# Batch 0's transforms in fp32, a first chunk fed with uncentred tokens, and staged weight sums in three buffers

## The chip, the cores and the metric

The kernel runs on one core of a Trainium2 chip. The metric is the device time of one execution in microseconds, lower is better. Three runs of the kernel before took 1044.42, 1047.3 and 1050.25 us, so its median is 1047.3 us.

## The reference, cut to what matters

Eight batches of 576 tokens with 512 channels. Pooled attention gives x; two Fourier transforms are added to it; an MLP on the normalised sum follows.

```python
k_p, v_p = means of k and v over 8 neighbouring tokens
x  = softmax(q @ k_p.T / sqrt(64)) @ v_p
u  = x + real(fft(fft(x, axis=tokens), axis=channels))
un = (u - mean(u)) / sqrt(var(u) + 1e-6)
out = u + relu(un @ w_ch1) @ w_ch2          # 512 -> 2048 -> 512
```

## The kernel before, in words

**MLP in blocks.** The 4608 tokens are cut into nine blocks of 512. The hidden layer has 16 chunks f of 128. Every operand is split into a high part of type fp32r and a low part, so a product is three fp32r matmuls (high by high, high by low, low by high). Blocks 0 and 1 are computed by `plain` (L889): per chunk twelve fp32r matmuls into `g` (L897), then a ReLU on ScalarE (L902), the low part `hl` on VectorE (L903) and twelve matmuls into `acc` (L861). Blocks 2 to 8 use a Strassen-like scheme with seven products per pair of chunks (L965).

**Front end.** `fe(b)` (L334) computes batch b up to the operands of its block: scores (`psS`, L440), softmax, transposes (`psT`, `psV`, `psR`), values (`psX`), then the two transforms by matmuls with cosine and sine tables. Sums `tmpE` (L618) and differences `tmpO` (L631) of mirrored tokens are split (`split`, L606 to L611), multiplied by `ca` (`psA` L652, `psB` L669), the results are split again (`parts`, `parts_last`, L635 to L642, and L658), and multiplied by `cb` (`psQ`, `psP`, L686). VectorE adds the results to x (L694, L695, L703, L704), forms the sum `s` (L715), the sums and differences U (L722, L723), and, with the mean from a matmul (`psM`, L763), the centred X (L770). `centre` (L727) makes the parts `un0h` on ScalarE (L732) and `un0l` on VectorE or POOL (L733). The lists UE and UL say how many of the four U operations and of the four low parts are on VectorE for batch 0, batch 1 and the others; the rest are on POOL.

**Weights.** The weights come as 64-bit numbers. `prep_w(n)` (L192) turns a piece into fp32 by two ScalarE operations (L203, L205) and one of VectorE (L208), then into its two parts (L215, L218); pieces are taken alternately from the two matrices. `HOLD` names for some pieces the instruction behind which ScalarE's part is queued. The weights of the first matrix are also written to the buffer `w1d` in device memory.

**Staged sums.** Blocks 2 to 8 need sums of neighbouring weight chunks. `load_pair(j)` (L231) brings chunks 2j and 2j+1 from `w1d` into one half of the buffer `sx`, `combine(j)` (L234) forms the sums by four VectorE operations (L238 to L241), splits them on ScalarE and POOL (L244, L245; the high parts go into the other half of `sx`), and writes them to `w1s`. Its last statement is `load_pair(j + 1)`, so a pair is loaded when the one before it has been written out:

```python
        if j + 1 < NFC // 2:
            load_pair(j + 1)
```

**Order.** A planner orders each engine's instructions by its own times; from position 86 of the main loop on, TensorE's order is the order of the program. Positions count the steps of `fast()`. The lists AT1 to AT7 say at which position each step of the front ends of batches 1 to 7 is issued, PAIRS at which a `combine` is. The two loads of `ca` and `cb` are issued on POOL's queue early in batch 0. `keep_busy` puts matmuls on TensorE whose result is not used (L325): 4 after batch 0's values and 5 after its mean.

Of the kernel before, what the change touches and what calls it, by code (L numbers as in the profile page):

```python
# [41 lines left out]

HZ = {0, 1}

DG = {0, 1}


UE = [4, 4, 2]
UL = [3, 3, 2]

AHEAD, WBUFS, LOOK = 10, 12, 9
HOLD = {0: ("B", 0), 1: ("S", 1, 0, 0), 2: ("S", 1, 0, 1), 4: ("T", 1, 0), 6: ("R", 1, 0), 8: ("S", 1, 1, 0), 10: ("S", 1, 1, 1)}
# [3 lines left out]
UNITS0, UNITS, TAIL = 90, 104, (2, 8, 14, 20, 26)  # L56
MANUAL = 86
PAIRS = [95, 110, 119, 136, 136, 145, 158, 174]
# [34 lines left out]
def tile_kernel(ctx: ExitStack, tc: tile.TileContext, qt, kt, vm, vr, w1, w2, cad, cbd, mkd, out):  # L93
# [20 lines left out]
    ss = cb[:, 1450:2890].rearrange("p (a n) -> p a n", a=5)  # L114
    mk = cp.tile([P, 5], F32, name="mk")
# [34 lines left out]
    for t in kpb:  # L150
        nc.gpsimd.memset(t, 0.0)
    for t in rw:
        nc.scalar.copy(out=t, in_=zz[:96, :P])
    nc.scalar.copy(out=xe, in_=zz[:, :290])

    for _ in range(4):
        nc.tensor.matmul(warm, lhsT=zz[:, 0:P], rhs=zz[:, 0:512], start=True, stop=True)

# [13 lines left out]
    highs = {}  # L172
# [19 lines left out]
    def prep_w(n):  # L192
# [3 lines left out]
        if wide:  # L196
            st = staged.pop(n)
            hi = st[:, :, :, 1]
            d0 = wd[3 * i + f % 3]
            di = d0.bitcast(I32).rearrange("p (r x) -> p r x", r=2)  # L200

            with tc.issue_after(behind[HOLD[n]].ins) if n in HOLD else ExitStack():
# [4 lines left out]
            with tc.issue_after(behind["Bv" if n < 3 else "C", 0].ins) if n < 6 else ExitStack():  # L207
                nc.vector.scalar_tensor_tensor(out=di, in0=hi, scalar=3, in1=di, op0=ALU.logical_shift_left, op1=ALU.bitwise_or)  # L208
        else:
            d0 = staged.pop(n)  # L210
        if i == 0:
# [5 lines left out]
        with queued(("C", 0) if n < 6 else None):  # L217
            nc.vector.tensor_tensor(out=lw, in0=d0, in1=raw(wh), op=ALU.subtract)  # L218
# [11 lines left out]

    def load_pair(j):  # L231
        nc.sync.dma_start(sx[:, 0:2 * DM].rearrange("p (f n) -> p f n", f=2), w1d[:, 2 * j:2 * j + 2])

    def combine(j):  # L234

        x, y = sx[:, 0:DM], sx[:, DM:2 * DM]
# [5 lines left out]
        for n, t in enumerate((x, y)):  # L242
            h = sx[:, (2 + n) * DM:(3 + n) * DM]
# [4 lines left out]
        if j + 1 < NFC // 2:  # L248
            load_pair(j + 1)
# [70 lines left out]
    def keep_busy(ins, n):  # L320

        with tc.issue_after(ins.ins):
            ps = bank(0, "idle")
            for _ in range(n):
                nc.tensor.matmul(ps, lhsT=ident, rhs=raw(ca)[:, 0:512], start=True, stop=True)  # L325
# [8 lines left out]
    def fe(b):  # L334
# [35 lines left out]
        def prep_k(g):  # L370
            ks = wk.tile([P, J], F32, tag="ks", name="ks")
            kb = kpb[g % 2]
            with queued({(1, 0): ("f", 0), (1, 1): ("f", 0)}.get((b, g))):
                total(ks, st["k", g], PK)
            with tc.issue_after(behind["R", 0, 0].ins) if b == 1 and g == 3 else ExitStack():
# [3 lines left out]
        def prep_rem(gi):  # L379
            vt = wk.tile([32, D], F32, tag="vt", name="vt")  # L380
# [3 lines left out]
        def prep_v(gi, i):  # L384
# [771 lines left out]
```

## Time and profile before

| | |
|---|---|
| median of three runs | 1047.3 us |
| the profiled execution | 1051.85 us |
| its span, first to last instruction | 1050.1 us, 1.75 us less |
| mean granted TensorE clock | 0.981 of 2.4 GHz |
| TensorE busy | 1003.6 us |
| VectorE, ScalarE, POOL busy | 692.2, 566.7 and 440.7 us |

Engine names in the rows: PE is TensorE's matmul, PEld its weight load, DVE is VectorE, ACT is ScalarE, POOL is GpSimd, SP the queue that issues most transfers. A stretch of the table of windows is given from the span's start in us. A busy PE is a modelled figure. The granted clock is 1.00 at 2.4 GHz and 0.50 at 1.2 GHz. A matmul on fp32 operands has two records, one on fp32r has one.

### The profile page before, as it was taken

The numbers are of one execution on the slowest core, as the hardware profiler recorded it, in microseconds if no ns is written. First come the engines' busy times: TensorE is split into PE (matmuls) and PEld (weight loads), VectorE is DVE, ScalarE is ACT, GpSimd is POOL, SyncE is SP. The second block draws the span as 40 slices with busy tenths as digits, with TensorE's granted clock in tenths as the row PEclk, the third lists the DMA queues.
The fourth block names the chain that finished last, engine by engine and source line by source line (L and its number), as shares of the span: only waits on it lengthen the run. The fifth ranks groups of instructions, "written<-read, shape, count | busy, mean of one in ns | idle before, by whom it ended". The sixth has DMA issues, their size and how long they took to land.

```text
span 1050.1 us, 18757 instructions
## 1 busy us (share of the span) xinstructions
PE 1003.6 (96%) x5982; PEld 866.0 (82%) x5982; DVE 692.2 (66%) x1387; ACT 566.7 (54%) x1687; POOL 440.7 (42%) x461
## 2 busy tenths in 40 slices
PE   7869999899889999999999999999999999999998
PEld 4547778677768799897899889998989988999897
DVE  6798686676579657965787668756875686223222
ACT  5769673556455756665567556755664344222222
POOL 5623333246533563556435743554351234222221
PEclk8989999899899999999999999999999999999999
DMA  7579997678856777878678757876787578888884
GB/s 272 183 227 390 374 320 257 197 256 254 258 153 188 232 256 207 259 234 279 189 235 275 256 186 231 284 230 213 219 258 215 174 237 286 274 256 263 288 257 135
DMA packets 161458, 256.11 MB, mean 244 GB/s; under 512 B 15952, under 2 KB 73296, under 8 KB 161104
## 3 DMA queue, kind: packets, MB, share of 16 engines
q1 hardware_dynamic: 161072, 252.24, 75.0%
q0 software_dynamic: 288, 2.66, 0.7%
q8 instruction: 49, 0.80, 0.3%
q14 instruction: 49, 0.40, 0.1%
HBM read 217.63 MB, written 37.22 MB: 243 GB/s over the span
## 4 chain that ended last, share of the span: by engine, by line
PE 76%; DVE 9%; DMA 7%; ACT 3%; POOL 2%; issue 2%; SPq 1%; DVEq 0%; POOLq 0%; ACTq 0%
PE acc L861 33%; PE x L965 23%; PE g L897 6%; PE psX L524 3%; PE psS L440 3%; DMA sx<-w1d 2%; PE psP L686 2%; DMA w1s<-sx 2%; PE psA L652 1%; ACT t L447 1%; PE psT L476 1%; PE psB L669 1%; PE psQ L686 1%; DMA v<-in_vm 1%; DMA k<-in_kt 1%
## 5 line engine op out<-in xcount | busy, mean ns | idle before, releaser
L926 DVE TENSOR_TENSOR sx<-x,sx 128x256 f32<-128x256 f32 x336 | 154.7, 464 | 163.3 <-PE x L965 153.1
L936 POOL TENSOR_TENSOR hl<-sx,hh 128x512 fp32r<-128x512 f32 x112 | 150.8, 1347 | 225.7 <-ACT hh L935 184.0
L965 PE MATMUL x<-un0h,w1op 128*128 128x256 f32 x896 | 173.6, 282 | 2.1 <-ACT U L527 1.6
L861 PE MATMUL acc<-hh,w2low 128*128 128x512 f32 x576 | 165.2, 400 | 0.0
L934 ACT ACTIVATE sx<-sx 128x512 f32<-128x512 f32 x112 | 71.0, 634 | 165.7 <-DVE sx L926 163.3
L965 PEld LDWEIGHTS x<-un0h,w1op 128*128 128x128 f32 x896 | 143.0, 189 | 14.9 <-ACT U L527 2.3
L965 PE MATMUL x<-un1h,w1op 128*128 128x256 f32 x672 | 135.0, 283 | 1.2 <-DVE sx L926 1.1
L965 PEld LDWEIGHTS x<-un1h,w1op 128*128 128x128 f32 x672 | 111.2, 189 | 13.6 <-DVE sx L926 2.0
L861 PEld LDWEIGHTS acc<-hh,w2low 128*128 128x128 f32 x576 | 101.6, 190 | 16.1 <-issue 0.4
L861 PE MATMUL acc<-hh,w2high 128*128 128x512 f32 x360 | 104.7, 398 | 1.1 <-ACT hh L935 1.1
L861 PE MATMUL acc<-hl,w2high 128*128 128x512 f32 x360 | 103.0, 395 | 0.0
L965 PE MATMUL x<-un0l,w1op 128*128 128x256 f32 x448 | 88.4, 279 | 0.0
L447 ACT ACTIVATE t<-psS,mx 128x72 f32<-128x72 f32 x240 | 74.3, 337 | 12.7 <-DVE mx L442 12.2
L861 PEld LDWEIGHTS acc<-hh,w2high 128*128 128x128 f32 x360 | 63.1, 189 | 11.1 <-ACT hh L935 1.8
L861 PEld LDWEIGHTS acc<-hl,w2high 128*128 128x128 f32 x360 | 63.2, 189 | 10.2 <-DVE w2low L218 0.4
L935 ACT CAST hh<-sx 128x512 fp32r<-128x512 f32 x112 | 69.7, 623 | 2.8
L965 PEld LDWEIGHTS x<-un0l,w1op 128*128 128x128 f32 x448 | 68.1, 188 | 0.0
L965 PE MATMUL x<-un1l,w1op 128*128 128x256 f32 x336 | 66.5, 279 | 0.0
L368 POOL TENSOR_TENSOR v<-v 128x256 f32<-128x256 f32 (+1 forms) x56 | 52.9, 945 | 30.6 <-DMA v<-in_vm 29.6
L456 POOL TENSOR_TENSOR t<-t,sm 128x720 f32<-128x720 f32 x30 | 44.9, 1499 | 43.3 <-DVE sm L455 11.7
L861 PE MATMUL acc<-hl,w2h 128*128 128x512 f32 x216 | 61.0, 402 | 0.0
L861 PE MATMUL acc<-hh,w2h 128*128 128x512 f32 x216 | 59.3, 395 | 0.0
(267 smaller groups left out, 2085.1 us busy)
## 6 DMA issues: line engine op xcount, KB each, us to landing
w1op<-w1s SPq DMA_DIRECT2D x224, 256.0 KB, 3.4
w1op<-w1p SPq DMA_DIRECT2D x200, 256.0 KB, 3.6
w2low<-w2l SPq DMA_DIRECT2D x128, 256.0 KB, 3.5
w2high<-w2d SPq DMA_DIRECT2D x80, 256.0 KB, 3.6
U<-in_w SPq DMA_DIRECT2D x16, 512.0 KB, 6.1
sx<-in_w SPq DMA_DIRECT2D x16, 512.0 KB, 6.0
w1s<-sx SPq DMA_DIRECT2D x32, 256.0 KB, 3.6
k<-in_kt SPq DMA_DIRECT2D x28, 288.0 KB, 3.7
```

The source lines that it names most:

```text
L368: nc.gpsimd.tensor_tensor(out=out if n == 1 else src[:, :, 0:n], in0=src[:, :, 0] if n == 1 else src[:, :, 0:n], in1=src[:, :, 1] if n == ...
L440: nc.tensor.matmul(ps[:, c * W2J:(c + 1) * W2J], lhsT=q[:, r0:r0 + P], rhs=kpb[g % 2], start=True, stop=True)
L447: behind["S", b, gi, i] = nc.scalar.activation(t[:, c0 + c, h], pv[:, c, h], AF.Exp, bias=mx[x], accum_out=sm[x])
L456: ins = nc.gpsimd.tensor_tensor(out=t, in0=t, in1=sm.unsqueeze(3).broadcast_to([P, 5, 2, J]), op=ALU.mult)
L686: nc.tensor.matmul(ps, lhsT=w, rhs=a, start=(i == 0), stop=(i == 6))
L861: nc.tensor.matmul(acc[e], lhsT=a[:, e], rhs=h, start=(f == 0 and x == 0), stop=(f == NFC - 1 and x == 2))
L897: nc.tensor.matmul(ps, lhsT=w[:, c], rhs=x[:, ti], start=(n == 0), stop=(n == 11))
L926: nc.vector.tensor_tensor(out=o, in0=x, in1=y, op=ALU.add)
L934: nc.scalar.activation(c, c, AF.Relu)
L935: nc.scalar.copy(out=h, in_=c)
L936: nc.gpsimd.tensor_tensor(out=l, in0=c, in1=raw(h), op=ALU.subtract)
L965: nc.tensor.matmul(ps, lhsT=w[:, q, i], rhs=y[:, c + i], start=(n == 0), stop=(n == 5))
```

## The change

- Batch 0's transforms (`NF`): the sums and differences of tokens go into the matmuls as fp32, with fp32 tables `cf` and `sf` that are loaded in the place of `ca` and `cb`. Both splits are gone; 30 fp32 matmuls in tiles of 96 tokens take the place of 74 fp32r ones: nine for `psA` (three of them with 128 columns), six for `psB`, six for `psQ`, nine for `psP`. Six ScalarE copies bring the results of the first transform to SBUF. The loads of `ca` and `cb` are issued at position 7 of the main loop instead.
- The first chunk of block 0 (`WHOLE = 1`): its weights stay whole in fp32 and are multiplied by U, the tokens with their mean on, by four fp32 matmuls; a fifth one takes the mean off: the sums of the weights over channels (`ws`, one VectorE reduction, and `psW`, one small matmul) times the token sums `s`.
- `KB = [4, 0]`: the five idle matmuls after batch 0's mean are gone.
- `UE` from [4, 4, 2] to [2, 3, 2] and `UL` from [3, 3, 2] to [0, 3, 2]; of the two L618 additions of batch 0 one goes to POOL (`FP`).
- Staged sums: pairs are loaded into six 512-column tiles, which give three places; three pairs are loaded ahead; the high parts have two places in `sx`.
- One of batch 1's four softmaxes (`SMX`) takes its exponentials straight from PSUM with ScalarE's own sums: VectorE's two subtractions (L449) and one reduction (L453) become ScalarE operations.
- Conditions of the order: L208 of the first three pieces waits for batch 0's last L631 instead of L637; eight `PINS`; five entries of AT3 four positions earlier, five of AT2 one earlier, five of PAIRS one later.

Renamed tiles and parts that are only moved are left out of this cut:

```diff
+SMX = {(1, 1, 0)}
+FP = {(0, 1)}
+PINS = [
+    ('Activation', 'un0h3', 0, 't3_1', 6),
+    ('DVE', 'hl', 12, 'AB2_1', 1),
+    ('DVE', 'nt2', 1, 'al3_2', 0),
+    ('DVE', 'xe', 2, 'rw1', 6),
+    ('DVE', 'sm1_1', 0, 'w2low', 3),
+    ('Activation', 'wdh', 0, 'wh1_3', 2),
+    ('Pool', 'wlo3_0', 0, 't3_0', 0),
+    ('Activation', 'wf3_3', 0, 'rw1', 7),
+]
+LEAD = 3
+KB = [4, 0]
-UE = [4, 4, 2]
-UL = [3, 3, 2]
+NF = {0}
+WHOLE = 1
+STEP = 96
+CONSTS = 7
+UE = [2, 3, 2]
+UL = [0, 3, 2]
-PAIRS = [95, 110, 119, 136, 136, 145, 158, 174]
+PAIRS = [95, 110, 119, 137, 137, 146, 159, 175]
-AT3 = [-46, -40, -37, -33, -33, -20, -18, -15, -15, -7, -7, -7, -7, 13, 13, 13, 13, 15, 15, 17, 18, 21, 21, 21, 21,
+AT3 = [-46, -40, -37, -33, -33, -24, -22, -19, -19, -11, -7, -7, -7, 13, 13, 13, 13, 15, 15, 17, 18, 21, 21, 21, 21,
...
-AT2 = [-6, 6, 8, 8, 8, 17, 18, 21, 22, 23, 24, 26, 27, 27, 29, 31, 32, 34, 35, 38, 39, 42, 43, 43, 44, 44, 52, 52,
-       52, 57, 59, 60, 61, 61, 61, 63, 65, 66, 70, 70, 70, 78, 78, 78, 78, 78, 80, 99]
+AT2 = [-6, 6, 8, 8, 8, 17, 18, 21, 22, 23, 24, 26, 27, 27, 29, 31, 32, 34, 35, 38, 38, 41, 42, 43, 44, 44, 52, 52,
+       52, 57, 59, 60, 61, 61, 61, 63, 64, 65, 70, 70, 70, 78, 78, 78, 78, 78, 80, 99]
...
     def prep_w(n):
...
+        if i == 0 and f < WHOLE:
+            ws = wk.tile([P, P], F32, tag="wf", bufs=2, name=f"ws{f}")
+            with queued(ORB.get(n)):
+                nc.vector.tensor_reduce(out=ws, in_=d0.rearrange("p (c m) -> p m c", m=P), op=ALU.add, axis=AX.X)
+            ps = bank(0, f"psW{f}")[:, 0:P]
+            nc.tensor.matmul(ps, lhsT=raw(avg), rhs=ws, start=True, stop=True)
+            nc.scalar.mul(wm[:, f], ps, -1.0)
...
+    halves = [(wd[0], wd[1]), (wd[3], wd[4]), (wd[2], wd[5])]
     def load_pair(j):
-        nc.sync.dma_start(sx[:, 0:2 * DM].rearrange("p (f n) -> p f n", f=2), w1d[:, 2 * j:2 * j + 2])
+        for n, t in enumerate(halves[j % 3]):
+            nc.sync.dma_start(t, w1d[:, 2 * j + n])
     def combine(j):
-        x, y = sx[:, 0:DM], sx[:, DM:2 * DM]
+        x, y = halves[j % 3]
...
-            h = sx[:, (2 + n) * DM:(3 + n) * DM]
+            h = sx[:, (2 * (j % 2) + n) * DM:(2 * (j % 2) + n + 1) * DM]
...
-        if j + 1 < NFC // 2:
-            load_pair(j + 1)
+        if j + LEAD < NFC // 2:
+            load_pair(j + LEAD)
...
+        def full(kind, n, dst, src, mat):
+            for i in range(3):
+                m = 97 if i == 2 and n == 258 else STEP
+                s0 = i * STEP
+                ps = bank(b, f"ps{kind}{b}_{i}")[0:m, 0:n]
+                nc.tensor.matmul(ps, lhsT=src[:, 0, s0:s0 + m], rhs=mat[:, 0], start=True, stop=False)
+                if n == 258:
+                    nc.tensor.matmul(ps[:, 1:256:2], lhsT=xz[:, s0:s0 + m], rhs=xcf, start=False, stop=False)
+                nc.tensor.matmul(ps, lhsT=src[:, 1, s0:s0 + m], rhs=mat[:, 1], start=False, stop=True)
+                behind["B", b] = nc.scalar.copy(out=dst[i][0:m], in_=ps)
...
         def seq(ps, src, last, n, l0, m, mat):
+            if nf:
+                w = csf if n == 258 else ssf
+                for i in range(3):
+                    k = 97 if i == 2 and n == 258 else STEP
+                    nc.tensor.matmul(ps, lhsT=src[0][i][0:k, l0:l0 + m], rhs=w[0:k, i], start=(i == 0), stop=(i == 2))
+                return
...
     def plain(k, acc, todo):
+            if k == 0 and f < WHOLE:
+                w = whole_w.pop(f).rearrange("p (c m) -> p c m", m=P)
...
+                        nc.tensor.matmul(p, lhsT=wm[:, x], rhs=sums[0][:, 0:BLK], start=True, stop=False)
+                for n, ti in enumerate((E0, O0, E1, O1)):
+                    nc.tensor.matmul(ps, lhsT=w[:, n], rhs=Us[0][:, ti, 0:BLK], start=False, stop=(n == 3))
...
     def fast():
         acc, todo = yield from plain(0, None, [])
-        load_pair(0)
+        for j in range(LEAD):
+            load_pair(j)
...
+        if pos == CONSTS:
+            with tc.issue_after(behind["t", 1 if ("t", 1) in behind else 0].ins):
+                load_consts()
```

## Rows read from the trace of the kernel before

**Rows 1.** Stretches: us; busy of PE, PEld, DVE, ACT, POOL; granted clock, DMA share, GB/s.

```profile
36.00:76.40 40.40, 28.46 (x146) 19.16 (x144) 39.39 (x78) 26.35 (x66) 17.92 (x20) 0.95 0.50 156
...
83.00:187.90 104.90, 104.90 (x485) 82.21 (x484) 76.99 (x135) 67.79 (x155) 36.91 (x44) 1.00 0.92 327
...
264.90:270.20 5.30, 4.89 (x20) 4.29 (x21) 2.37 (x5) 1.17 (x4) 4.50 (x7) 0.50 0.83 250
...
340.00:1045.00 705.00, 696.54 (x4521) 626.60 (x4520) 436.92 (x890) 357.83 (x1062) 299.21 (x294) 1.00 0.76 238
```

**Rows 2.** What TensorE waited for: us in total, times, longest; 76 to 340 us.

```profile
PE g L897 <- DVE un0l L733: 5.6, 1, 5.6
...
PE psA L652 <- ACT f L608: 3.6, 1, 3.6
PE psS L440 <- DVE U L704: 2.3, 1, 2.3
```

**Rows 3.** VectorE's groups from 36 to 76.4 us: shapes, count; busy us, mean ns; idle before.

```profile
L723 DVE TENSOR_TENSOR U<-X,U 128x288 f32<-128x288 f32 x4 | 1.6, 438 | 0.0
...
L610 DVE TENSOR_TENSOR f<-tmpO,f 128x288 fp32r<-128x288 f32 x2 | 1.4, 748 | 0.0
...
L733 DVE TENSOR_TENSOR un0l<-X,un0h 128x288 fp32r<-128x288 f32 x3 | 1.2, 437 | 0.0
...
L610 DVE TENSOR_TENSOR f<-tmpE,f 128x290 fp32r<-128x290 f32 x2 | 0.9, 508 | 0.0
...
L453 DVE TENSOR_REDUCE sm<-t 128x10 f32<-128x720 f32 x1 | 0.9, 884 | 0.0
...
L637 DVE TENSOR_TENSOR B<-psB,B 128x256 fp32r<-128x256 f32 x2 | 0.8, 420 | 0.0
...
L628 DVE TENSOR_TENSOR xe<-U,xe 1x290 fp32r<-1x290 f32 x1 | 0.8, 814 | 0.6 <-ACT xe L627 0.6
...
L733 DVE TENSOR_TENSOR un0l<-X,un0h 128x224 fp32r<-128x224 f32 x2 | 0.7, 372 | 0.0
...
L449 DVE TENSOR_TENSOR t<-psS,mx 128x432 f32<-128x432 f32 x1 | 0.6, 589 | 0.0
...
L658 DVE SCALAR_TENSOR_TENSOR AB<-AB,mk,psA 2x258 fp32r<-2x258 f32 x1 | 0.5, 483 | 0.0
...
L642 DVE TENSOR_TENSOR AB<-psB,AB 32x256 fp32r<-32x256 f32 x1 | 0.4, 415 | 0.0
```

**Rows 4.** Timeline of POOL and of VectorE around 68 and 78 us: start, us, instruction.

```profile
67.64 1.08 POOL L733 TENSOR_TENSOR un0l<-X,un0h 128x288 fp32r<-128x288 f32 x1 [12.42 <-ACT un0h L732]
...
67.99 1.27 DVE L218 TENSOR_TENSOR w1low<-wdh,un1h 128x512 fp32r<-128x512 f32 x1
...
78.78 0.67 DVE L218 TENSOR_TENSOR w1low<-wdh,un1h 128x512 fp32r<-128x512 f32 x1
```

**Rows 5.** Timeline of TensorE in the start, from five stretches: values, transforms, idle matmuls, first chunks.

```profile
35.38 2.17 PE L524 MATMUL psX<-R,wlo 32*128 32x288 f32 x8
...
42.81 2.07 PE L652 MATMUL psA<-ca,f 128*128 128x258 f32 x12 [1.62 <-ACT f L608]
...
56.58 0.51 PE L686 MATMUL psQ<-cb,AB 96*128 96x288 f32 x2
...
61.84 4.45 PE L325 MATMUL idle<-ca,ident 128*128 128x512 f32 x10
...
88.49 1.09 PE L897 MATMUL g<-un0h,un1h 128*128 128x512 f32 x4
```

**Rows 6.** What VectorE waited for, 180 to 340 us: the loads of pairs.

```profile
DVE sx L238 <- DMA sx<-w1d: 11.1, 4, 3.2
...
DVE sx L238 <- DMA w1op<-w1p: 2.7, 1, 2.7
```

**Rows 7.** Timeline around 300 us: batch 3's last multiply on POOL, its first transposes.

```profile
299.56 1.39 POOL L456 TENSOR_TENSOR t<-t,sm 128x720 f32<-128x720 f32 x1 [0.89 <-PE g L897]
...
305.48 0.60 PE L476 MATMUL psT<-ident,t 128*128 128x128 f32 x4
```

More of the change, by code (lines that the diff above doesn't have):

```diff
@@ L171, in tile_kernel @@
     staged, lows = {}, {}
-    highs = {}
+    highs, whole_w, sums = {}, {}, {}
     def fresh(name):
@@ L216, in prep_w @@
         lw = fresh(f"w{i + 1}low")
[L217 removed]
+        with queued(LWB.get(n)):
             nc.vector.tensor_tensor(out=lw, in0=d0, in1=raw(wh), op=ALU.subtract)
@@ L320, in keep_busy @@
     def keep_busy(ins, n):
+        if not n:
+            return
         with tc.issue_after(ins.ins):
@@ L370, in prep_k @@
         def prep_k(g):
-            ks = wk.tile([P, J], F32, tag="ks", name="ks")
+            ks = wk.tile([P, J], F32, tag="ks", name=f"ks{b}_{g}")
             kb = kpb[g % 2]
-            with queued({(1, 0): ("f", 0), (1, 1): ("f", 0)}.get((b, g))):
+            with queued(FEQ.get(("k", b, g))):
                 total(ks, st["k", g], PK)
-            with tc.issue_after(behind["R", 0, 0].ins) if b == 1 and g == 3 else ExitStack():
+            with queued(FEQ.get(("kb", b, g))):
                 nc.scalar.mul(kb[0:64, 0:J], ks[0:64], 1.0 / 64.0)
@@ new lines, in fe @@
+        if nf:
+            a01 = raw(gt(0, f"A0_{b}"))
+            bf = raw(wk.tile([P, 1160], F32R, tag="ln0", name=f"B01_{b}"))
+            A2, B2 = 258, 256
+            AB = [[a01[:, 0:258], a01[:, 258:516], raw(gt(1, f"A1_{b}"))[:, 0:258]]] * 2 + [[bf[:, 256 * i:256 * i + 256] for i in range(3)]] * 2
+            full("A", 258, AB[0], ev, ccf)
+            yield
+            full("B", 256, AB[2], tmp, scf)
+            yield
+        else:
+            AB = [gt(0, f"A0_{b}"), gt(1, f"A1_{b}"), None, None, gt(4, f"AB2_{b}")]
+            A2, B2 = AB[4][:, 0:258], AB[4][:, 258:514]
+            for i, m in enumerate((P, P, 34)):
+                s0 = i * P
+                ps = bank(b, f"psA{b}_{i}")[0:m, 0:258]
+                mm = [(x[:, j, s0:s0 + m], cc[:, j, y]) for x, y in ((eh, 0), (el, 0), (eh, 1)) for j in range(2)]
+                mm.append((xe[:, s0:s0 + m], xc))
+                for n, (w, a) in enumerate(mm):
+                    nc.tensor.matmul(ps, lhsT=w, rhs=a, start=(n == 0), stop=(n == len(mm) - 1))
+                if i < 2:
+                    parts((AB[i],), ps, 258)
+                else:
+                    parts_last(A2, ps)
+                    nc.scalar.copy(out=A2[96:98], in_=ps[32:34])
+                    nc.vector.scalar_tensor_tensor(out=A2[96:98], in0=raw(A2[96:98]), scalar=mk[96:98, 4:5], in1=ps[32:34], op0=ALU.mult, op1=ALU.add)
+                if i == 1 or b and i == 2 or b > 1:
+                    yield
+            oh, ol = split((2, 3), tmp, HS)
+            B01 = wk.tile([P, 1160], F32R, tag="ln0", name=f"B01_{b}")
+            AB[2], AB[3] = B01[:, 0:512], B01[:, 512:1024]
+            for i, m in enumerate((P, P, 32)):
+                s0 = i * P
+                ps = bank(b, f"psB{b}_{i}")[0:m, 0:256]
+                mm = [(x[:, j, s0:s0 + m], sc[:, j, y]) for x, y in ((oh, 0), (ol, 0), (oh, 1)) for j in range(2)]
+                for n, (w, a) in enumerate(mm):
+                    nc.tensor.matmul(ps, lhsT=w, rhs=a, start=(n == 0), stop=(n == len(mm) - 1))
+                if i < 2:
+                    parts((AB[2 + i],), ps, 256)
+                else:
+                    parts_last(B2, ps)
+                if i != 1 or b > 1:
+                    yield
@@ L764, in fe @@
                 if b == 0 and cl.start:
-                    keep_busy(mean, 5)
+                    keep_busy(mean, KB[1])
             else:
@@ L1038, in tile_kernel @@
                 combine(j)
-        if pos in TAIL:
+        for _ in range(TAIL.count(pos)):
             next(fe0, None)
@@ L1046, in tile_kernel @@
             ctx.enter_context(tc.manual_schedule(engines={mybir.EngineType.PE}))
+    made = {}
+    for ins in nc.cur_bb.bb.instructions:
+        if ins.outs and getattr(ins.outs[0], "bass_ap", None) is not None:
+            name = ins.outs[0].bass_ap.tensor.name.rpartition("_")[0]
+            made.setdefault((str(ins.engine).rpartition(".")[2], name), []).append(ins)
+    order = mybir.DependencyInfo(mybir.DependencyClass.NoSync, mybir.DependencyReason.DATA)
+    for engine, first, m, then, n in PINS:
+        tc.add_manual_dep(made[engine, then][n], made[engine, first][m].name, order, reason="order")
 def _consts():
```

224 lines of the change are left out of this document (128 added, 96 removed).

## Prediction

> **What bounds the kernel now.** I read the table of windows first. In the long stretch from 340 us TensorE is busy for 696.5 of 705 us at full clock [rows 1]; almost nothing that the change touches lies there, so the time can only come from before 340 us. From 83 to 187.9 us TensorE is busy without a break as well. What is left are the start and two holes. In the start, from 36 to 76.4 us, VectorE is busy for 39.39 of 40.40 us and TensorE for 28.46 [rows 1], and the waits of TensorE name VectorE: 5.6 us in one piece for the low parts of the centred tokens [rows 2]. So VectorE's work sets when the dense stretch begins. The holes lie at 261 and 291 us: 3.6 us for batch 2's split and 2.3 us for an addition of VectorE [rows 2]. After the first, TensorE runs 5.30 us at 1.2 GHz, 4.89 of them busy [rows 1]; it had stood for 3.6 us. Why VectorE is late there is in its own waits: L238, the first operation of a combination, stood five times for its pair, 11.1 us in four waits and 2.7 in a fifth [rows 6]; everything behind it on VectorE stood with it.
>
> **The change, the start.** The splits of batch 0's transforms go from VectorE: L610 1.4 and 0.9 us, L637 0.8 and a twin alike, L642 0.4 and a twin alike, L628 0.8, L658 0.5, together 6.0 us. Four L723 go to POOL, 1.6 us. Of the low parts 1.2 and 0.7 us, and one more of 0.4 that follows the stretch, go too: 2.3 us. One L618 goes, 0.4 us by the mean of L723. The softmax that ScalarE takes over leaves out L449 with 0.6 us, its second form at two thirds of that, 0.4, and L453 with 0.9: 1.9 us [rows 3]. Sum 12.2 us. Against it stands the reduction of the weights; no row shows it, the nearest is L453, 0.9 us for 720 elements against 512, so I take 0.9. Net 11.3 us off VectorE.
>
> But eleven operations land on POOL (four L723, six low parts, one L618), each 1.08 us by POOL's own L733 [rows 4], 11.9 us. Beside that L733 an L218 of VectorE took 1.27 us; the same operation took 0.67 alone [rows 4]. So 1.08 us of POOL cost VectorE 0.60, or 0.56 for each us. Eleven operations then cost 6.7 us and VectorE's net gain is 4.6. Ends: nothing lost, if what runs beside POOL is not of that kind, 11.3; all of POOL's time lost, 11.3 - 11.9 = -0.6. I take the price that the row shows.
>
> The Trainium skill, page "SBUF — State Buffer", section "SBUF: two separate sides", says of VectorE with two SBUF inputs and GpSimd that they share a pair of ports under an exclusive lock: one of them "fully blocks". By that rule VectorE's gain would be the lower end, -0.6; the row shows about half of it, since the two only partly overlapped. It speaks against putting this work on POOL and is the first rival below.
>
> On TensorE the start gives nothing. Four fp32 matmuls of 288 columns took 2.17 us, 0.54 each [rows 5]; scaled by columns the new 30 cost 3.7 (`psA`), 2.9, 3.3 and 4.9 us, 14.8 together. The 74 old ones ran from 42.81 to 57.09 us, 14.3 us with their waits [rows 5]. What the missing splits save in waiting the slower matmuls give back: I count zero. If they start at 42.81 as before, they end 0.5 us later, which only matters if VectorE has run dry by then. The first chunk's five fp32 matmuls cost what the five idle ones did that are removed, 4.45 us for ten records [rows 5]. But they need neither the centred tokens nor the parts, so they lie where TensorE waited. Before, two groups of four matmuls, one of each of two chunks, had run when it stood still for the 5.6 us; now a whole chunk and one group have, two more groups of at most 1.09 us [rows 5]: 2.2 us. So the start gives 4.6 + 2.2 = 6.8 us, between 1.6 and 13.5. What is late next there are still the low parts, now on POOL.
>
> **The staging.** With three places a pair is loaded three combinations ahead, and L238 finds it. The waits of 13.8 us on VectorE [rows 6] are not all worth time: only where TensorE then stood. That is 3.6 and 2.3 us [rows 2] and half of the 4.89 us that ran at 1.2 GHz, 2.4: 8.3 us. The 2.7 us of the fourth wait are less than the hole of 3.6 us that follows; the step of AT2 that brings batch 2's values one position forward has to close the rest. The end below is 2.3, when the first hole stays; the end above 8.3, since I know no other stall that this would remove. Each pair is now two transfers on SP's queue, and the load of pair j+3 still waits there for the write of pair j, as before; five times instead of seven.
>
> **Counted at nothing.** The loads of `ca` and `cb` move into the stretch from 83 us. They are 2.66 MB (5204 columns of 512 bytes), 8.1 us at the 327 GB/s of that stretch, whose DMA share is 0.92 [rows 1]; its free 8% of 104.9 us, 8.4 us, just hides them. If not, the weights come up to 8.1 us later. On POOL's queue they now stand behind batch 1's multiply, and nothing of batch 1 needs them before its own transforms. The start has 1.48 MB of tables to load instead. ScalarE has 14 us free in the start for the exponentials that it takes over. The moved steps of AT2 and AT3 issue matmuls with their evictions and no transfers; the five combinations that come a position later bring four VectorE, two ScalarE and two POOL operations and their writes with them, a microsecond later. With the pins I count them at nothing, since they fall on engines with room; the price where they fail is the last rival's.
>
> **The sum.** 6.8 + 8.3 = 15.1 us off the profiled execution's 1051.85 us gives 1036.75. That execution stood 4.55 us above the median of the runs, so I predict 1032.2 us.
>
> **Rivals.** First, POOL takes back the start: VectorE stands for all of POOL's time. For it: the lengthened L218. Against: the new work beside it is partly from PSUM. Start 1.6, total 9.9, time 1037.4; chance 0.14. Second, the staging moves its wait: the hole at 261 us stays, because tables and sums of batch 2 are late for another reason, and only 2.3 us go. For it: the hole is longer than the wait before it. Against: VectorE was busy through that hole with work that the wait had pushed back. 6.8 + 2.3 = 9.1, time 1038.2; chance 0.12. Third, POOL costs VectorE nothing: 13.5 + 8.3 = 21.8, time 1025.5; chance 0.12. Fourth, on the other side: steps that come too early. From position 86 on TensorE's order is fixed, so a step brought forward stops it when its input is late. Place: the five steps of AT3 and five of AT2. Price: a hole like the one at 261 us with its slow stretch, 3.6 + 2.45 = 6.05 us each [rows 1, 2]. Two such places leave a gain, 15.1 us are gone at the third; from the fourth the kernel is over 0.5% slower: 1032.2 + 24.2 = 1056.4. For it: batch 3's transposes began at 305.48 us on data that POOL finished at 300.95 [rows 7]; 4.5 us of slack against four positions of at least 0.9 us each. Against: that slack holds, and VectorE runs ahead after the staging. Chance 0.07. That leaves 0.55 for the forecast.
>
> **The numbers.** Below 0.5%, 5.2 us, a measurement of this kernel can hardly tell a change: the three runs lie within 5.8. Faster by more means under 1042.1 us: all cases but the fourth reach it, less what lies at their edges; 0.85. Within 0.5%: 0.08, the tails of the first two. Slower: 0.07. Both low ends together, 1.6 + 2.3, give 1043.4; the third rival 1025.5, and the scatter of a median lies around both: 1021 to 1043. The likeliest case alone: 1027 to 1038.
>
> **What would show it.** Right: L238 waits for no load; TensorE has no hole at 261 and 291 us minus the shift; the dense stretch begins by 70 us; 30 fp32 matmuls take about 15 us. POOL's price is read from the lengths of L722 and L218 beside it. Wrong: a dense stretch that begins after 74 us, new waits of over 2 us on transposes of batch 3, a TensorE that waits for weights, or a granted clock of 0.50 in new places.

## The result and the profile after

| | median us | runs | ratio to the kernel before |
|---|---|---|---|
| the changed kernel | 1032.97 | 4, 1030.86 to 1037.91 | 0.9857, 95% 0.9822 to 0.9892 |
| the same, measured again | 1033.06 | 4, 1031.06 to 1035.93 | 0.9846, 95% 0.9821 to 0.9872 |

The kernel before, run beside them, has medians of 1046.9 us (4 runs) and 1049.55 us (11 runs). So the change makes the kernel faster by 14 to 16.5 us (the differences of the medians); 1032.2 us was predicted. The profiled execution of the changed kernel took 1030.86 us with a span of 1029.1 us, so it stands 2.1 us below its median, while that of before stood 4.55 us above its own. The two spans differ by 21.0 us, more than the medians do.

First the windows that answer to [rows 1], of the changed kernel (columns: busy us and instructions of TensorE, its weight loads, VectorE, ScalarE and POOL, then granted clock, DMA share, GB/s):

```profile
36.00:76.40 40.40, 38.08 (x155) 25.17 (x154) 36.28 (x64) 28.38 (x87) 30.03 (x32) 0.96 0.61 206
83.00:170.00 87.00, 87.00 (x407) 68.47 (x406) 59.21 (x106) 59.91 (x138) 25.89 (x35) 1.00 0.96 351
170.00:200.00 30.00, 23.35 (x103) 17.46 (x102) 27.13 (x56) 13.75 (x51) 15.41 (x18) 0.89 0.81 271
240.00:300.00 60.00, 58.01 (x308) 48.41 (x307) 43.78 (x79) 28.90 (x106) 28.22 (x37) 1.00 0.60 185
```

In the start TensorE is busy for 38.08 of 40.40 us instead of 28.46, and VectorE has a little room, 36.28 instead of 39.39. From 240 to 300 us TensorE is busy for 58.01 us at a clock of 1.00; the kernel before had in this window and in the one from 170 us

```profile
170.00:200.00 30.00, 27.26 (x115) 20.87 (x114) 20.60 (x43) 9.63 (x20) 9.50 (x9) 0.89 0.62 188
240.00:300.00 60.00, 53.51 (x278) 44.73 (x277) 39.06 (x82) 31.45 (x114) 36.28 (x45) 0.94 0.78 243
```

so both holes and the stretch at the lower clock have gone. But from 170 to 200 us, where block 1 begins in both kernels, TensorE is now busy for only 23.35 us instead of 27.26, at the same clock of 0.89. The waits of TensorE from 30 to 420 us (us in total, times, longest), which answer to [rows 2], say why:

```profile
PE g L1003 <- DVE X L877: 3.1, 1, 3.1
PE g L1003 <- ACT t L521: 2.6, 1, 2.6
PE g L1003 <- POOL un0l L840: 1.1, 2, 0.6
```

and of the kernel before, for the same place:

```profile
PE g L897 <- DVE X L770: 2.1, 1, 2.1
```

The 5.6 us for low parts have shrunk to 1.1 us. The longest wait is now 3.1 us for batch 1's centred tokens, where block 1 begins; the wait at this place took 2.1 us before. A second one, 2.6 us, follows at 192 us. The start itself, on TensorE's timeline (start, us busy, in brackets the idle time before and who ended it):

```profile
58.83 1.09 PE L1018 MATMUL g<-s,wm 128*128 128x512 f32 x2
59.76 3.60 PE L1021 MATMUL g<-U,w1whole 128*128 128x512 f32 x8
...
63.83 0.73 PE L1003 MATMUL g<-un0h,un1h 128*128 128x512 f32 x2
...
68.45 0.55 PE L1003 MATMUL g<-un0l,un1h 128*128 128x512 f32 x1 [0.56 <-POOL un0l L840]
...
70.51 1.85 PE L968 MATMUL acc<-hh,w2h 128*128 128x512 f32 x4
```

The whole chunk (L1018, L1021) fills 58.8 to 63.4 us. From 68.5 us on TensorE doesn't stand again until 176 us; before, the like began at 76.4 us.

**Landmarks.** Two profiled spans differ by more than the change, so I go by moments that every trace has. I read three from the lines of the first layer and of the products: when block 0's last group of low weights starts (`w1low`, last start; in the table, "block 0 ends"), when block 1 begins (`w1op`, first start), when block 2 begins (`x`, first start). These are the rows of the changed kernel (count; ns min, median, max; first and last start):

```profile
L1003 PE MATMUL g<-un0h,w1op x128: 387/393/796, 181.6 to 311.0; 128*128 128x512 f32 x128
...
L1003 PE MATMUL g<-un0h,w1low x60: 388/397/628, 68.8 to 172.5; 128*128 128x512 f32 x60
...
L1091 PE MATMUL x<-un0h,w1op x896: 275/281/388, 314.0 to 1014.9; 128*128 128x256 f32 x180
```

and those of the kernel before:

```profile
L897 PE MATMUL g<-un0h,w1op x128: 388/394/792, 190.9 to 329.4; 128*128 128x512 f32 x128
L897 PE MATMUL g<-un0h,w1low x64: 388/398/628, 79.2 to 184.7; 128*128 128x512 f32 x64
...
L965 PE MATMUL x<-un0h,w1op x896: 276/281/388, 332.5 to 1035.9; 128*128 128x256 f32 x180
```

All kernels of this study, read in the same way, in us, beside their measured ratio:

| kernel | block 0 ends | block 1 begins | block 2 begins | span | ratio (interval in the text) |
|---|---|---|---|---|---|
| before | 184.7 | 190.9 | 332.5 | 1050.1 | 1 |
| before_again | 184.4 | 190.7 | 331.8 | 1046.6 | one run |
| after | 172.5 | 181.6 | 314.0 | 1029.1 | 0.9857 |
| after_again | 173.5 | 182.6 | 315.5 | 1031.4 | 0.9846 |
| b_stage | 182.7 | 190.7 | 323.7 | 1038.1 | 0.994 |
| a_stage_old | 173.9 | 183.7 | 328.0 | 1046.0 | 0.9971 |
| a_whole0 | 181.3 | 190.6 | 325.9 | 1039.7 | 0.9967 |
| a_whole0p | 180.6 | 190.1 | 324.2 | 1043.6 | 0.9937 |
| a_nf0 | 179.0 | 194.0 | 330.0 | 1049.2 | 1.004 |
| a_nopool | 172.5 | 182.8 | 317.9 | 1032.3 | 0.9895 |
| a_steps_old | 173.5 | 182.5 | 319.6 | 1034.8 | 0.9848 |
| a_psp | 174.5 | 181.3 | 316.2 | 1030.4 | 0.9843 |
| a_at2 | 172.8 | 181.9 | 319.1 | 1034.0 | 0.9904 |
| a_best | 172.8 | 178.7 | 315.6 | 1030.6 | 0.9867 |

Means of the two profiles each: block 0 ends 11.6 us earlier, block 1 begins 8.7 us earlier (190.8 to 182.1), and the stretch from there to block 2 is 8.7 us shorter (141.35 to 132.65). Behind that nothing is left of the change: from block 2 to the end of the span the two profiles of before need 717.6 and 714.8 us, those after 715.1 and 715.9.

### The profile page after: what moved, and what is told of

The parts are those of the page before. It is cut to its first block, busy times and chain, and to the rows that moved or that the text cites. A ratio compares the mean times of both kernels' runs of the same rounds, so it can differ in the third digit from the quotient of the medians.

```text
span 1029.1 us, 18705 instructions
## 1 busy us (share of the span) xinstructions
PE 999.2 (97%) x5958; PEld 861.9 (84%) x5958; DVE 689.1 (67%) x1360; ACT 564.1 (55%) x1701; POOL 449.2 (44%) x477
## 4 chain that ended last, share of the span: by engine, by line
PE 75%; DVE 9%; ACT 7%; DMA 3%; POOL 3%; issue 2%; SPq 0%; DVEq 0%; ACTq 0%; POOLq 0%
PE acc L968 32%; PE x L1091 23%; PE g L1003 6%; PE psX L598 3%; ACT t L521 2%; PE psS L514 2%; PE psP L793 2%; PE psQ L793 1%; PE psA L753 1%; PE psT L550 1%; PE psB L770 1%; DMA k<-in_kt 1%; DVE X L854 1%; DVE U L992 1%; DMA vr<-in_vr 1%
## 5 line engine op out<-in xcount | busy, mean ns | idle before, releaser
L521 ACT ACTIVATE t<-psS,mx 128x72 f32<-128x72 f32 x250 | 77.0, 330 | 10.4 <-DVE mx L516 9.9
L968 PEld LDWEIGHTS acc<-hh,w2high 128*128 128x128 f32 x360 | 62.8, 188 | 11.6 <-ACT hh L1061 1.6
L851 POOL TENSOR_TENSOR un1l<-X,un1h 128x256 fp32r<-128x256 f32 (+11 forms) x26 | 32.3, 1243 | 63.6 <-ACT un1h L850 63.6
```

The costliest lines, as they stand in the source:

```text
L521: behind["S", b, gi, i] = nc.scalar.activation(t[:, c0 + c, h], pv[:, c, h], AF.Exp, bias=mx[x], accum_out=sm[x])
L851: e.tensor_tensor(out=l, in0=x, in1=raw(h), op=ALU.subtract)
L968: nc.tensor.matmul(acc[e], lhsT=a[:, e], rhs=h, start=(f == 0 and x == 0), stop=(f == NFC - 1 and x == 2))
```

## Experiments

Before the experiments the theory was the forecast's: 6.8 us from the start, 8.3 from the staging, nothing from the rest. In each run one part is undone or done alone. Each quotes what was on record before it ran.

**The same programs again.** No edit.

> The changed kernel once more, on the chip of the other runs of this set: 1032 to 1035 us, a ratio of 0.986 to the kernel before. It gives the base for the three runs beside it, and a second profile of the same program: what of the gaps at 178 and 192 us is there again belongs to the program, what is not to one execution.

> The kernel before once more, for a second profile of the same program: 1042 to 1052 us. The start and the two holes at 261 and 291 us, with L238 waiting four or five times for its pair, belong to the program if they are there again; block 1 should begin at 190 to 192 us and block 2 at 330 to 334 us. If the hole at 261 us and the slow stretch behind it are missing, they were of one execution, and the forecast's 8.3 us for the staging rested on it; then block 2 begins 3 to 6 us earlier.

Measured: 0.9846 (0.9821 to 0.9872) for the changed kernel, with a gap of 3.1 us again where block 1 begins and one of 1.6 us, followed by 1.7 us at the variance, where 2.6 and 0.5 stood. The kernel before took 1048.36 us in its one run; L238 waited again, by the view of its line (idle time until what, us and times):

```profile
  DMA sx<-w1d: 10.8, 4
  DMA w1op<-w1p: 2.6, 1
```

and TensorE stood behind it, by its timeline:

```profile
265.13 1.96 PE L652 MATMUL psA<-ca,f 128*128 128x258 f32 x6 [3.00 <-ACT f L608]
...
290.61 0.73 PE L440 MATMUL psS<-kpb,q 128*128 128x144 f32 x4 [1.71 <-DVE U L704]
```

So the start, these waits and the two holes belong to the program. The landmarks of either program repeat within 1.5 us; the stretch behind block 2 scatters by up to 2.8.

**Staging alone, and all but the staging.** `b_stage` is the kernel before with the changed `load_pair` and `combine` and three pairs asked for ahead; `a_stage_old` is the changed kernel with the old ones:

```diff
-    halves = [(wd[0], wd[1]), (wd[3], wd[4]), (wd[2], wd[5])]
...
-        if j + LEAD < NFC // 2:
-            load_pair(j + LEAD)
+        if j + 1 < NFC // 2:
+            load_pair(j + 1)
```

> The kernel before with the staging of the change alone: three places, each pair asked for three combinations ahead, the two parts in sx. By the forecast the waits of L238 for loads go and with them the holes at 261 and 291 us: 8.3 us off, a ratio of 0.992, about 1038.6 us. By the second rival (the first hole stays for another reason) 2.3 us off, 0.998, 1044.6 us. If the hole at 346 us hung on the same queue too, as the trace after the change lets one think, 10 to 11 us off, 0.990, 1036 us.

> The changed kernel with the staging of before: one place, each pair asked for by the combination before it. By the forecast 8.3 us come back, about 1041.3 us, a ratio to the kernel before of 0.9935, with holes of TensorE of over 2 us near 240 and 270 us. By the second rival 2.3 us, 1035.3 us, 0.988. If VectorE, with less to do in the start, now reaches the combinations earlier, the waits are as long or longer and the loss is 8.3 or more.

Measured: `b_stage` 0.994 (0.9917 to 0.9963), 6.3 us off, between 3.9 and 8.7. L241, its first operation of a combination, waits for no load. The window of `b_stage` from 240 to 300 us:

```profile
240.00:300.00 60.00, 58.09 (x307) 48.13 (x305) 35.45 (x73) 31.32 (x114) 27.53 (x38) 1.00 0.61 186
```

58.09 us busy at full clock. The stretch from block 1 to block 2 shrinks from 141.35 to 133.0 us, 8.35 us: the forecast's term, in its place. The second rival, that the first hole stays, is out. The wait of block 2's products for ScalarE, 1.65 us at 346 us in the kernel before, stays in this kernel with 1.8 us, so the third number of the expectation is out too.

`a_stage_old` 0.9971 (0.9953 to 0.9989): about 12.6 us worse than the changed kernel, more than the staging gains alone. VectorE's waits for its pair are longer than in the kernel before, 15.0 us against 11.1 [rows 6], by the view of the combination's first line:

```profile
  DMA sx<-w1d: 15.0, 4
```

On TensorE's timeline three gaps stand behind them:

```profile
246.20 0.40 PE L595 MATMUL psX<-R,rw 96*128 96x288 f32 x1 [4.15 <-DVE R L579]
...
277.80 0.61 PE L790 MATMUL psQ<-cb,AB 96*128 96x288 f32 x1 [2.23 <-DVE AB L719]
...
295.44 0.40 PE L872 MATMUL psM<-shl,avg 128*128 128x288 f32 x1 [2.16 <-DVE shl L822]
```

They are 4.15, 2.23 and 2.16 us long. The size is that of the third theory of the expectation, a loss of 8.3 us or more, but its reason isn't borne out: VectorE is ready for each of the first six pairs later than in the kernel before, by 1.7 to 7.6 us. These are the first and the last start of a combination, in the kernel before and then in `a_stage_old`:

```profile
172.38 0.41 DVE L238 TENSOR_TENSOR sx<-sx 128x256 f32<-128x256 f32 x1
...
288.57 0.43 DVE L238 TENSOR_TENSOR sx<-sx 128x256 f32<-128x256 f32 x1 [3.17 <-DMA sx<-w1d]
```

```profile
177.44 0.42 DVE L296 TENSOR_TENSOR sx<-sx 128x256 f32<-128x256 f32 x1
...
286.77 1.60 DVE L296 TENSOR_TENSOR sx<-sx 128x256 f32<-128x256 f32 x1
```

The first begins 5.1 us later, the last 1.8 us earlier, while block 1 begins 7.1 us earlier (183.7 against 190.8). Each pair is loaded only when the one before has been written out, so I read the eight combinations as a chain with a pace of its own, 15.6 us a pair (16.6 before). It ends within 2 us of the same time in both kernels, and what hangs on VectorE waits for it. So without the staging the start's gain is mostly lost again, with 3.0 us left (0.9971). Why the first combination begins later here I didn't settle.

**The whole chunk.** `a_whole0` sets WHOLE to 0. `a_whole0p` does the same with three orders set by hand, after the trace of `a_whole0` showed ScalarE and POOL standing for loads in a new order:

```diff
-WHOLE = 1
+WHOLE = 0
...
+    ('Activation', 'U2', 0, 'U2', 3), ('Activation', 'R1_0', 1, 'U2', 2),
+    ('Pool', 'un0l0', 7, 'v1_1', 0),
```

> The changed kernel with the first chunk of block 0 in high and low parts again; the whole chunk, the sums of its weights and their matmul go. By the forecast TensorE loses 2.2 us of work that it had ahead of the parts: 1035.2 us, a ratio to the kernel before of 0.988. If the low parts on POOL set the pace, TensorE stands from about 59 us, where the whole chunk began, for the first of them and the loss is all of its 4.5 us: 1037.5 us, 0.990. If VectorE's reduction of the weights and the wait for it cost as much as the whole chunk gives, no change.

> The changed kernel with the first chunk in high and low parts again, as in the run before, with two orders set by hand: on ScalarE the unpacking of the first weights comes ahead of that of a later piece and the copies of R ahead of the next piece, on POOL the four subtractions and the low parts come ahead of the value sums of v1. In the run before, ScalarE stood 3 us for a piece of weights and POOL 3 us for v, and TensorE 4.0 us behind them. If those two waits made the 9 us that block 1 came later, this run loses no more than the forecast's 2.2 us against the changed kernel, about 1035 us; if the whole chunk itself is worth what it takes, 4.5 us, about 1037.5 us; if the waits only take another place, 1042 us or more again.

Measured: 0.9967 (0.9945 to 0.9988) and 0.9937 (0.9916 to 0.9958), 12 and 9 us worse than the changed kernel. All losses expected of the first were too small. In the second the waits did take another place: ScalarE still stands 2.65 us for a piece of weights, ahead of copies that the scores need, and TensorE 3.00 us behind it. The timeline of `a_whole0p`, one row of ScalarE and four of TensorE:

```profile
58.14 0.67 ACT L253 ACTIVATE wdh<-U 128x512 int32<-128x512 uint8 x1 [2.65 <-DMA U<-in_w]
...
59.16 1.81 PE L514 MATMUL psS<-kpb,q 128*128 128x144 f32 x6 [3.00 <-ACT R L578]
...
66.43 1.19 PE L1003 MATMUL g<-un0h,un1h 128*128 128x512 f32 x4 [0.17 <-ACT un0h L839]
...
82.70 1.95 PE L968 MATMUL acc<-hl,w2h 128*128 128x512 f32 x4 [2.57 <-DVE hl L1028]
84.45 1.91 PE L1003 MATMUL g<-un0h,un1h 128*128 128x512 f32 x4
```

The first chunk begins at 66.43 us, when the changed kernel has finished one and begun the next (63.83). And a place that I had not counted: at 82.70 us the second layer waits 2.57 us for `hl`, and the matmuls behind it are slow at first (the four at 84.45 take 1.91 us, four of the same kind at 87.15 1.10; the granted clock from 76.4 to 100 us is 0.93, in the changed kernel 1.00). With the whole chunk the second layer's first group is ready at 70.51 us, right behind the next chunk. But `hl` was late by VectorE's order: its input `hh` was ready by 78.4 us, and operations on weights and on batch 1's softmax stood in front of it until 81.97 us:

```profile
77.37 1.06 ACT L1027 ACTIVATE hh<-g 128x512 fp32r<-128x512 f32 x2
...
81.97 0.68 DVE L1028 SCALAR_TENSOR_TENSOR hl<-g,hh 128x512 fp32r<-128x512 f32 x1
```

Block 0 ends 7.6 us later (180.6 against 173.0) and block 1 begins 8.0 us later. The wait behind the weights, 3.0 us, and that for `hl`, 2.57 us, may both be of the order and not of the chunk, so the whole chunk is worth something between 2.0 and 7.6 us at block 0's end.

**The transforms.** `a_nf0` sets NF to the empty set: batch 0's transforms in parts, `ca` and `cb` loaded in the start. One entry of PINS counts one `xe` more; the rest is as changed.

```diff
-NF = {0}
+NF = set()
...
-        nc.gpsimd.dma_start(cf[:, 0:2026], cfd)
-        nc.gpsimd.dma_start(sf[:, 0:864], sfd)
+        nc.gpsimd.dma_start(ca, cad)
+        nc.gpsimd.dma_start(cb, cbd)
```

> The changed kernel with batch 0's transforms in high and low parts again (their tables ca and cb loaded in the start as before); the whole chunk, the work on POOL, the staging and the moved steps stay. By the forecast TensorE needs as long for either and VectorE has 6.0 us of splits again, in a start where it set the end: up to 6 us slower than the changed kernel, 1039 us. If TensorE and the waits behind it set the start now and VectorE has slack, 0 to 2 us, 1034 us. If the whole chunk alone made the gain, block 1 begins within 2 us of where it does in the changed kernel.

Measured: 1.004 (1.0024 to 1.0055), 20 us worse than the changed kernel and worse than the kernel before; no theory had that. In the start it is as the forecast has it: block 0 ends 6.0 us later (179.0 against 173.0), VectorE is busy for 39.75 of the 40.40 us from 36 us, and the transforms take from 41.74 to 57.2 us. Another 9 us are lost behind: 5.9 where block 1 begins, at 194.0, 15.0 us after block 0's mark against 9.1 in the changed kernel, and 3.4 up to block 2 (136.0 against 132.65). The timeline of `a_nf0`, three rows of TensorE and two of VectorE:

```profile
186.26 2.26 PE L870 MATMUL psM<-s,avg 128*128 128x288 f32 x4 [3.11 <-DVE s L822]
194.03 1.19 PE L1003 MATMUL g<-un0h,w1op 128*128 128x512 f32 x2 [5.50 <-ACT sx L305]
...
202.03 1.22 PE L1003 MATMUL g<-un0l,w1op 128*128 128x512 f32 x2 [4.02 <-DVE un0l L840]
...
184.60 1.52 DVE L822 TENSOR_TENSOR s<-X 128x288 f32<-128x288 f32 x1
...
188.18 1.48 DVE L300 TENSOR_TENSOR wdl<-wdh,wdl 128x256 f32<-128x256 f32 x1
```

VectorE's order has changed with the edit: between batch 1's additions (L810, L829), its sum (L822) and its centring (L877) it now does operations of the combinations (L300 to L302), one of them 1.48 us long, and ScalarE has their copies (L305) in front of the high parts. TensorE waits 3.1, 5.5 and 4.0 us in that chain, and the granted clock from 170 to 200 us is 0.75. So I put 9 of the 20 us down not to the transforms, but to an order that the edit brought along. Another 3.7 us lie behind block 2 (719.2 us against 715.5), somewhat more than the 2.8 us by which the two executions of the kernel before differ there.

**The work on POOL.** `a_nopool` takes back what POOL got in batch 0:

```diff
-FP = {(0, 1)}
+FP = set()
-UE = [2, 3, 2]
-UL = [0, 3, 2]
+UE = [4, 3, 2]
+UL = [4, 3, 2]
```

> The changed kernel with all that it gives to POOL in batch 0 back on VectorE: four L830, six low parts and one L692. By the forecast's price, 0.56 us of VectorE for each us of POOL, VectorE takes on 4.3 us of work and loses 6.7 us of contention: 2.4 us faster, about 1030.6 us. By the first rival (VectorE stands for all of POOL's time) 11.9 - 4.3 = 7.6 us faster, 1025.4 us. If POOL costs VectorE nothing, 4.3 us slower, 1037.3 us. A fourth view, from the trace after the change: TensorE waits twice for low parts that POOL writes one after another in 9.4 us, so VectorE would give them sooner, and the dense stretch would begin before 68.5 us whatever the price.

Measured: 0.9895 (0.9871 to 0.9919), 4.6 us worse than the changed kernel. The forecast's price (2.4 us faster) and the first rival (7.6 us faster) are out; the value is that of the third rival, but not by its mechanism. TensorE runs without a break from 67.4 us on, 1.1 us earlier, as the fourth view had it, but block 0's mark is the same 172.5 us, and block 1 begins 0.7 us later. The loss that this trace shows, 3.1 us at block 2, lies mostly behind that: from block 1 to block 2 it takes 135.1 us instead of 132.65, with waits of TensorE of 1.6 us for block 1's low parts at 188 us and 1.7 us for a variance at 216 us (0.5 us in the changed kernel). Why the operations of batch 0 matter there I didn't settle. The profiled execution (1034.11 us) was the fastest of six, 4.2 us under their median, so the rest of the loss is not in the trace.

The price itself can be read. POOL's low parts ran without a break, and beside them VectorE's operations with two inputs in SBUF took longer than the same ones in `a_nopool` (groups of POOL and of VectorE, busy us and mean ns; first the changed kernel):

```profile
L840 POOL TENSOR_TENSOR un0l<-X,un0h 128x288 fp32r<-128x288 f32 (+2 forms) x9 | 9.4, 1078 | 0.0
L830 POOL TENSOR_TENSOR U<-X,U 128x288 f32<-128x288 f32 x4 | 4.7, 1210 | 4.7 <-DVE U L829 4.7
...
L276 DVE TENSOR_TENSOR w2low<-wdl,w2h 128x512 fp32r<-128x512 f32 x1 | 1.3, 1287 | 0.0
...
L877 DVE TENSOR_TENSOR X<-U,psM 128x576 f32<-128x576 f32 x1 | 0.7, 742 | 0.0
```

and the same groups of VectorE in `a_nopool`:

```profile
L877 DVE TENSOR_TENSOR X<-U,psM 128x576 f32<-128x576 f32 x1 | 0.7, 735 | 0.0
...
L276 DVE TENSOR_TENSOR w2low<-wdl,w2h 128x512 fp32r<-128x512 f32 x1 | 0.7, 670 | 0.0
```

L276 took 1.29 instead of 0.67 us, but L877, which reads PSUM, 0.74 and 0.735. The seven operations of that kind (L256, L276, L888) from 62.7 to 70.1 us took 7.5 us together instead of 4.8: 2.7 us lost. Two more lie outside this window: L256 at 60.65 us, 0.84 instead of 0.67, beside a low part, and L709 at 40.10 us, 0.85 instead of 0.44, beside the L692 that went to POOL. That makes 3.3 us in all. POOL loses as well: in `a_whole0p` two low parts beside L877 took 0.78 us each, the six behind them 1.07.

The Trainium skill, page "SBUF — State Buffer", section "SBUF: two separate sides", has the pair of ports held for a whole instruction while the other engine is fully blocked. By that rule these seven operations (4.8 us alone) and the six and a half low parts that POOL did beside them from 62.7 to 69.5 us (5.1 us at 0.78) would take 9.9 us one after another, an estimate; VectorE's took 7.5. The measurement decides: each holds the other up, but neither for the whole of the other's time.

**The moved steps.** `a_steps_old` has PAIRS, AT2 and AT3 as before:

```diff
-PAIRS = [95, 110, 119, 137, 137, 146, 159, 175]
+PAIRS = [95, 110, 119, 136, 136, 145, 158, 174]
```

and five entries each of AT2 and AT3 likewise.

> The changed kernel with the steps of batches 2 and 3 and the combinations where they were before. By the forecast, which counts the moved steps at nothing, 1033 us. By the fourth rival the moved steps cost time, and this is faster by 6 us for a place, 1027 us or less. If the steps of batch 2 were moved to where the new order needs them, it is slower: a gap of 2 to 3 us with its slow stretch, about 1037 us.

Measured: 0.9848 (0.9822 to 0.9875) against 0.9846: no difference within some 3 us. Its profile, taken in the longest of its runs (1036.6 us), has block 2 begin at 319.6 us, 4.1 and 5.6 us later than the two profiles of the changed kernel. Its other runs, 1033.1 to 1033.9 us, don't bear that out, so a landmark of a single trace can be off by more than the 1.5 us above. The fourth rival is out, and no gain of the moved steps shows either.

**Three tries to go further.** They aim at the two gaps between 176 and 200 us. `a_psp` sets the first of these orders, `a_at2` moves two steps of AT2, `a_best` does both and sets the second order too:

```diff
+    ('PE', 'psP1_2', 6, 'g1_0_15', 0),
+    ('PE', 'psM1', 1, 'acc0_0', 43),
...
-AT2 = [-6, 6, 8, 8, 8, 17,
+AT2 = [-6, 6, 8, 10, 11, 17,
```

> The changed kernel with one more order: batch 1's last inverse transform goes ahead of the last chunk's matmuls of block 0. The chain from it to block 1's first matmul (addition, sum, mean, centred tokens, high part) then begins some 3 us earlier. If this chain makes the gap of 3.1 us at 178 us, the gap and the slow matmuls behind it go: 3 to 5 us faster than the changed kernel, about 1029 us, a ratio of 0.982. If VectorE is what is late there, the chain stands for it and nothing is won: 1033 us.

> The changed kernel with the second group of scores of batch 2 two and three positions later. In the changed kernel 14 score matmuls come in one go at 189.7 us, take the free banks of PSUM, and block 1's second chunk waits 1.6 to 2.6 us until ScalarE's exponentials give one back. If the banks are what is missing, this wait and that of the variance behind it (0.5 to 1.7 us) go: 3 us faster, 1030 us, a ratio to the kernel before of 0.982. If ScalarE and VectorE are late there anyway, the wait moves to the scores' own users (transposes of batch 2) and nothing is won: 1033 us.

> The same, and batch 1's last inverse transform ahead of the last chunk's matmuls of block 0 and the two means ahead of the low half of its second layer. Both gaps between 176 and 200 us should go: block 1 begins 2 to 3 us earlier than 182 us and its second chunk does not wait, 5 to 6 us faster than the changed kernel, 1028 us, 0.980. If what comes behind (splits of batch 2 at 280 us) then is late, as after the order of the last inverse transform alone, half of it or less is left, 1031 us.

Measured: 0.9843 (0.9819 to 0.9868), 0.9904 (0.9877 to 0.9931), 0.9867 (0.9839 to 0.9894). None beats the changed kernel, and `a_at2` comes out some 5 us slower. In `a_psp` the gap in front of block 1 is still 2.6 us. In `a_best` it has shrunk to 1.7 us and block 1 begins at 178.7 us, 3.4 us earlier, but block 2 at 315.6 as in the changed kernel. The waits have moved. Of TensorE, from 30 to 420 us, in `a_at2`:

```profile
PE g L1003 <- DVE hl L1028: 3.7, 1, 3.7
...
PE psS L514 <- ACT t L521: 2.0, 1, 2.0
```

and in `a_best`:

```profile
PE psA L753 <- DVE f L684: 2.7, 2, 1.6
...
PE g L1003 <- DMA wdl<-w1d: 1.7, 1, 1.7
```

With the scores later, the chunk's `hl` and the scores' own bank are what TensorE waits for, 3.7 and 2.0 us; with block 1 earlier, batch 2's split (2.7 us), and the clock from 240 to 280 us is 0.91 in `a_best` instead of 1.00. What a smaller gap in front gave was lost again in waits for VectorE and ScalarE behind it.

## Why the prediction was right, and where it was not

**The total.** 15.1 us were predicted, 14 to 16.5 us measured. The landmarks give 8.7 for the start and 8.7 for the staging, 17.4; the difference to the medians is about the scatter behind block 2. The staging is right by its mechanism. That the start fits too is in part luck: block 0 ends 11.6 us earlier where the forecast's terms come to 6.8, and 2.9 us that it had not counted are given back behind that.

**The start, 6.8 us: the direction right, one term mis-sized, one loss left out.** The dense stretch begins at 68.5 us, before the 70 us that I named. Of the terms:
- *The splits*, 6.0 us, hold: in `a_nf0`, which has them again, block 0 ends 6.0 us later than in the changed kernel.
- *All the rest*, 6.8 - 6.0 = 0.8 us, was too small: `a_nf0`, which has the chunk and the work on POOL without the fp32 transforms, ends block 0 5.5 us earlier than before (179.0 against 184.55).
- *POOL's price*, 6.7 us for eleven operations at 0.60 each, is the term that was mis-sized. The size of one was right (1.29 against 0.67 us), the count was not: only where VectorE has two inputs in SBUF beside such an operation is time lost, and that was 3.3 us. Beside the four L830 VectorE's operations kept their 0.44 us, and it was POOL that took longer, 1.18 us each instead of 0.79. In `a_nf0` VectorE's L829, L256, L276 and L888 beside POOL's took 3.9 us longer than the same ones in `a_nopool`, so this explains 2.8 of the 4.7 us that the rest lacks there; where the other 1.9 come from stays open.
- *Work ahead of the parts*, 2.2 us: between 2.0 and 7.6 us by `a_whole0p`, so it is neither shown nor refuted.
- *What the relief is worth.* The forecast takes each us off VectorE as one off the start. But VectorE is no longer what comes last all the way: from 36 to 76.4 us it stands for 4.1 us (40.40 less 36.28) instead of 1.0, most of it for ScalarE's part of the first weights and for POOL's L830. Two of its waits from 30 to 80 us in the changed kernel:

```profile
DVE w1whole L256 <- ACT w1whole L253: 2.3, 1, 2.3
DVE X L877 <- POOL U L830: 1.5, 2, 0.8
```

  So how the 11.6 us divide among the relief, the chunk and POOL can't be said from these runs beyond the 6.0 and 5.5 us above.
- *What is late next*: the low parts on POOL, as said, twice 0.56 us. What I had not followed is the end of block 0: batch 1's chain of sum, mean and centring is fixed in place there. Its centred tokens come 3.1 us after TensorE has run dry instead of 2.1, and batch 1's last inverse-transform matmuls now stand behind block 0's last group. Together 2.9 of the 11.6 us are given back (11.6 to 8.7).

**The transforms on TensorE, 0.** From 40.20 to 53.94 us they took 13.7 us, with one transpose of 0.27 us among them; 14.8 were predicted and the old ones took 14.3. Their length is right. But they began 2.6 us earlier than the old ones (40.20 against 42.81), in part because TensorE no longer stands 1.62 us for the split [rows 5], and so ended 3.1 us earlier, where the forecast had them end 0.5 us later.

**The staging, 8.3 us.** Right in place and size: 8.35 us by the landmarks of `b_stage`, whose time, 6.3 us (3.9 to 8.7), allows it. In the changed kernel the same stretch is 8.7 us shorter, but `a_nopool` shows that it depends on more than the staging. L299, the first line of a combination there, waits for no load, the holes at 261 and 291 us have no successor over 1 us, and the clock between 240 and 300 us is 1.00.

**Counted at nothing.** The tables `ca` and `cb` come in while TensorE is busy for 87.00 of 87.00 us from 83 to 170 us, so they are hidden. The moved steps cost and gain nothing that `a_steps_old` could show.

**The rivals.** Price of POOL for all its time: out, by `a_nopool`. The first hole stays: out, by `b_stage`. POOL free of charge: out by the lengths, 3.3 us, which lie halfway between it and my price; its 1025.5 us wasn't reached. Steps too early: out, by `a_steps_old`; its mechanism did show in `a_best`, where TensorE got ahead of batch 2's split.

**What the parts are worth together.** Undone one at a time they cost 20 (transforms), 12.6 (staging), 9 (whole chunk) and 4.6 us (POOL), 46 us in a change that gives 15. Two places show why the sum is too large: in `a_nf0` 9 of 20 us lie at block 1 and behind it, where VectorE's order has changed; in `a_stage_old` the chain of pairs ends when it did before, so the start's gain is lost with the staging's. My reading is that the parts share one order of VectorE, which fits one set of arrival times; no run tests that by itself.

## What to carry to other kernels

Follow the chain to the next engine before you take what an engine is relieved of as time saved: VectorE got its relief here and then stood 3 us more, for ScalarE and POOL. A chain of load, work and write with one place can keep its own pace, and then a gain in front of it is lost until more places free it. A part undone inside a tuned order measures the order too, so read how far the landmark just behind the part moved before taking the whole time as its price. And a gap closed on TensorE is worth something only if the engines behind it in the chain are early enough: here they weren't, and moving the gaps gave nothing.

## What I had not expected of the hardware

VectorE and POOL hold each other up, but not by whole instructions: 0.67 to some 1.2 us on VectorE and 0.78 to 1.07 on POOL, while VectorE's L877 and L516, which read PSUM, were hardly longer (0.74 us against 0.735, 0.518 against 0.512). Which of the two pays differs: beside the L829 and L822 POOL's L830 took longer in the changed kernel, 1.18 us each, and VectorE kept its 0.44; in `a_whole0p` both paid, L829 with 1.04 us and L830 with 0.99. And two executions of one program agreed within 1.5 us up to block 2 and then differed by up to 2.8 us in the 715 us behind it (717.6 and 714.8), so a difference of two profiled spans, 21.0 us here, says less than the landmarks do.
